# Raw-weight loads issued by ScalarE behind the upper-half copy, and a later place for the second block's first conversion step

## Chip, cores and metric

One core of one Trainium2 chip runs the whole kernel in one launch. The metric is the device time of one execution in microseconds (us).

## What is computed

```python
attn_out = _attn_ref(q, k, v)              # [2, 8, 576, 64]: pooled attention (factor 4) repeated, plus attention in a band |i-j| < 4
x = attn_out as [1152, 512]
h = x @ w_in; r = max(h, 0); g = s*r*r + b # d_ff = 2048
x = g @ w_out                              # [1152, 512]
p = probs / (sum(probs) + 1e-9)
for e in range(4):                         # d_ff = 1024 for each expert
    out += p[:, e:e+1] * (max(x @ w1[e], 0) @ w2[e])
```

The weights w_in and w_out of the first feed-forward network reach the kernel as pairs of 32-bit words, the bits of 64-bit floating-point numbers; the kernel makes 32-bit numbers of them.

## The kernel before

The work falls into three stages. The **attention** runs in 16 units, 4 groups of tokens by 4 pairs of heads, and each unit passes through a chain of short steps on several engines. The **first network** runs in four blocks (n = 0 to 3) of 512 columns of d_ff, the second in eight. TensorE does every large product as three products of fp32r parts: an upper part (a rounded copy) and a lower part (what the copy lost).

A unit's steps, with the lines: TensorE transposes q (L512), ScalarE copies it (L519 `qz`), VectorE pools it (L526 `qd`). TensorE computes the scores (L576 to L614), VectorE the row maxima (L615, L617), ScalarE the exponentials with their sums (L571, `exps`). VectorE normalises (L630 to L635), TensorE transposes the result (L657), ScalarE copies it (L660 `pT`), and TensorE multiplies by the values (L678 with the pooled values `vd`, L685). ScalarE and VectorE add the two results (L694 `ud`, L701 `xg`), ScalarE makes the upper part of x (L713) and GpSimd the lower one (L715; VectorE for the last unit of a group). `xg` has one buffer, so a unit's L701 waits for the previous unit's L713 and L715. GpSimd also pools the values (L474, L475). The steps of the units overlap: while one unit's exponentials run, the previous one is normalised and transposed.

From the fourth unit on, TensorE takes pieces of block 0 of the first network between these steps (`take_slot`); their results go through `L767` on ScalarE, `L769` on VectorE, `L772` on ScalarE and `L773` on VectorE. In the first ten units TensorE also multiplies a tile of zeros (L361, L584, `keep_warm`). The number of these multiplications is fixed in the program.

**Conversions.** Each block of the first network takes four quarters of weights, two of w_in and two of w_out, 1 MB each as raw words. `load_next` (L100) takes the next quarter from a list and issues its load into one of two `raw` buffers. A conversion (`prep`, L143) of a quarter has seven instructions over tiles of 128x1024: `magnitude` (L157, ScalarE), `clamp` (L161, VectorE), `join` (L167 and L175, VectorE), `sign` (L186, VectorE, the last reader of the raw words), `high` (L196, ScalarE) and `low` (L199, VectorE). The last two of a quarter are interleaved with the steps of the next one (`tail`, L203). There are 16 conversions, counted here from 1; conversions 1 to 4 serve block 0, 5 to 8 block 1. The first two loads are issued at the start; in the kernel before, `low` then calls `load_next`, which issues on SyncE's queue. A third load therefore waits until conversion 1's `sign` has read its raw buffer.

On every engine but GpSimd a scheduler sets the order of the instructions from the order in which the program issues them and from their priorities, so an edit at one place can move instructions at others. Each engine then runs its own list in order.

Of the kernel before, what the change touches and what calls it, by code (L numbers as in the profile page):

```python
# [8 lines left out]
F32 = mybir.dt.float32  # L9
# [3 lines left out]
ACTF = mybir.ActivationFunctionType  # L13
# [9 lines left out]
def attn_moe_moe_kernel(  # L23
# [14 lines left out]
    nc = tc.nc  # L38
# [40 lines left out]
    def f32(ap):  # L79
        return ap.bitcast(F32)  # L80
# [16 lines left out]
    tail = []  # L97
    pools = {}

    def load_next():  # L100
        if not stream:
            return
        n, which, half = stream.pop(0)
        wi, wo, f0 = blocks[n]
        m = 2 if n < n_moe1 else 1
        dt = I32 if n < n_moe1 else F32
        if n < n_moe1:
            wi, wo = wi.bitcast(I32), wo.bitcast(I32)
        f0 += half * 256
        if which == 0:  # L110
            src = wi[:, f0 * m : (f0 + 256) * m].rearrange("(k p) f -> p k f", p=P)
        else:
            src = wo[f0 : f0 + 256, :].rearrange("(c p) d -> p c d", p=P)
        if n < n_moe1:
            t = rawp.tile([P, 2048], dt, tag="raw", name="raw")
        else:
            if "raw2" not in pools:
                t = rawp.tile([P, 2048], dt, tag="raw", name="raw2")
                pools["raw2"] = [t[:, :1024], t[:, 1024:]]
            t = pools["raw2"].pop(0)  # L120
            pools["raw2"].append(t)
        nc.sync.dma_start(out=t.rearrange("p (a b) -> p a b", a=src.shape[1]), in_=src)
        raw[n, which, half] = t


# [2 lines left out]
    def w_slot(which):  # L128
        i = places[which].pop(0)
        places[which].append(i)  # L130
        if i < 3 - which:
            pool = wp1 if which else wp0
        else:
            pool = pools["wy" if which else "wx"]
        return [
            pool.tile([P, 1024], F32R, tag=f"w{which}{c}{i}", name=f"w{which}{c}", bufs=1)
            for c in range(2)
        ]

    def prep(n, which, half):  # L140

        if n >= n_moe1:
            return prep2(n, which, half)  # L143
        parts = w_slot(which)
        wt[n, which, half] = parts
        st = {}

        def words():
            w = raw[n, which, half].rearrange("p (n two) -> p n two", two=2)
            return w[:, :, 0], w[:, :, 1]  # L150

        def magnitude():
            f = rawp.tile([P, 1024], F32, tag="cv", name="cv")
            st["f"] = f
            nc.scalar.activation(out=f, in_=words()[1].bitcast(F32), func=ACTF.Abs)  # L157

        def clamp():
            f = st["f"]  # L160
            nc.vector.tensor_scalar(  # L161
                out=f, in0=f, scalar1=2.0**-15, scalar2=122879.9921875, op0=ALU.max, op1=ALU.min
            )

        def join():
            c = st["f"].bitcast(I32)
            nc.vector.tensor_scalar(  # L167
                out=c,
                in0=c,
                scalar1=5,  # L170
                scalar2=2,
                op0=ALU.logical_shift_left,
                op1=ALU.logical_shift_right,
            )
            nc.vector.scalar_tensor_tensor(  # L175
                out=c,
                in0=words()[0],
                scalar=29,
                in1=c,
                op0=ALU.logical_shift_right,  # L180
                op1=ALU.bitwise_or,
            )

        def sign():
            c = st["f"].bitcast(I32)
            nc.vector.scalar_tensor_tensor(  # L186
                out=c,
                in0=words()[1],
                scalar=-(2**30),
                in1=c,  # L190
                op0=ALU.bitwise_and,
                op1=ALU.bitwise_or,
            )

        def high():
            nc.scalar.copy(parts[0], st["f"])  # L196

        def low():
            nc.vector.tensor_tensor(  # L199
                out=parts[1], in0=st["f"], in1=f32(parts[0]), op=ALU.subtract  # L200
            )
            load_next()
            ready.add((n, which, half))  # L203


        nonlocal tail
        steps = [magnitude] + tail[:1] + [clamp] + tail[1:] + [join, sign]
        tail = [high, low]
        return steps

# [5 lines left out]
    def prep2(n, which, half):  # L216
# [10 lines left out]
        def done():  # L227
            load_next()
            ready.add((n, which, half))
# [118 lines left out]
    nc.vector.memset(idle, 0.0)  # L348

    last_pe = {}  # L350
    firsts = []

    def take_slot():
# [44 lines left out]
    def unit(u):  # L398
        g, j = divmod(u, NP)
        b, hf = divmod(g, HALVES)  # L400
        return g, j, b, hf
# [149 lines left out]
    def b_step(u):  # L551

        g, j, b, hf = unit(u)
# [14 lines left out]
        sm = sums[u % 2]  # L568

        def exps(out, ps, m, total):  # L570
            nc.scalar.activation(  # L571
                out=out, in_=ps, func=ACTF.Exp, bias=m, scale=1.0, accum_out=total
            )

# [41 lines left out]
        for a in range(len(pooled)):  # L616
            nc.vector.tensor_reduce(  # L617
                out=md[:, a], in_=pooled[a], axis=AX.X, op=ALU.max, negate=True
# [372 lines left out]
    for i in range(last + 1):  # L991
# [36 lines left out]
        if i < 2:  # L1028
            load_next()
# [104 lines left out]
```

## Time and profile before

| | |
|---|---|
| median of 3 runs | 686.23 us (685.72 to 687.32) |
| the profiled execution | 685.9 us |
| its span, first to last instruction | 684.1 us |
| TensorE busy | 673.0 us (98%) |
| VectorE busy | 404.7 us (59%) |
| ScalarE busy | 345.2 us (50%) |
| GpSimd busy | 103.0 us (15%) |

The time outside the span, 1.8 us, lies before the first and after the last instruction. Busy shares are means over the whole span; a stretch at the start may look quite different.

### The profile page before, as it was taken

The page shows a single profiled execution, that of the slowest core. Times are in us where ns is not written, and L with a number is a line of the kernel's source. Part 1 is how long each engine was busy: PE and PEld are TensorE (multiplying, and loading weights), DVE is VectorE, ACT ScalarE, POOL GpSimd, SP SyncE. Part 2 cuts the span into 40 slices and gives each one's busy share as a digit, 9 for nine tenths or more (in the row PEclk, how much of TensorE's full clock was granted, in tenths as well). Part 3 has the DMA queues.
Part 4 walks back from the last instruction along what each step waited for, and adds up shares of the span by engine and source line. Part 5 has one row for each costly group of instructions (what it writes and reads, how often), then busy time and mean ns, then how long its engine had stood idle before and what let it go on. Part 6 is the DMA issues. An engine that isn't in the chain of part 4 may idle for free.

```text
span 684.1 us, 11957 instructions
## 1 busy us (share of the span) xinstructions
PE 673.0 (98%) x4788; PEld 614.5 (90%) x4788; DVE 404.7 (59%) x720; ACT 345.2 (50%) x846; POOL 103.0 (15%) x123
## 2 busy tenths in 40 slices
PE   9879999999999999999999999999999999999997
PEld 6668888999999999999899998898998999988996
DVE  1899878598834425695525645646456365455442
ACT  3777788787956656754443433334234234343220
POOL 4431540100002001021201201210112012010000
PEclk9999999999999999999999999999999999999999
DMA  9975845133500101000301201101102012011012
GB/s 189 229 173 112 145 130 157 63 120 127 184 1 1 32 1 62 1 32 0 86 9 61 63 31 32 62 32 61 32 32 65 29 32 92 27 36 32 1 62 77
DMA packets 54167, 46.43 MB, mean 68 GB/s; under 512 B 32224, under 2 KB 42720, under 8 KB 54112
## 3 DMA queue, kind: packets, MB, share of 16 engines
q1 hardware_dynamic: 54112, 45.67, 24.5%
q8 instruction: 37, 0.61, 0.4%
q14 instruction: 18, 0.15, 0.1%
HBM read 43.31 MB, written 2.36 MB: 67 GB/s over the span
## 4 chain that ended last, share of the span: by engine, by line
PE 89%; DVE 7%; ACT 2%; issue 1%; POOL 1%; POOLq 0%; ACTq 0%
PE psm L316 43%; PE psx L863 26%; PE psx L316 13%; PE psa L361 2%; PE psa L591 1%; PE psa L657 1%; DVE cv L175 1%; PE psa L685 1%; PE psa L512 1%; DVE cv L167 1%; PE psa L494 1%; PE psa L678 1%; DVE cv L186 1%; DVE cv L161 0%; DVE pl L632 0%
## 5 line engine op out<-in xcount | busy, mean ns | idle before, releaser
L316 PE MATMUL psm<-w,h 128*128 128x512 f32 x864 | 208.7, 391 | 0.0
L316 PEld LDWEIGHTS psm<-w,h 128*128 128x128 f32 x864 | 158.5, 188 | 30.0
L863 PE MATMUL psx<-x,w 128*128 128x320 f32 (+1 forms) x768 | 117.7, 296 | 0.0
L863 PEld LDWEIGHTS psx<-x,w 128*128 128x128 f32 x768 | 109.2, 189 | 1.7
L259 POOL TENSOR_TENSOR sw<-raw 128x256 f32<-128x256 f32 x32 | 30.1, 960 | 412.1 <-DMA raw<-in_moe_w_dram 270.3
L878 ACT COPY r<-psx 128x320 f32<-128x320 f32 (+1 forms) x96 | 38.1, 396 | 92.9 <-PE psx L863 92.5
L881 ACT ACTIVATE h<-r 128x320 fp32r<-128x320 f32 (+1 forms) x96 | 42.1, 444 | 82.8 <-DVE r L892 82.8
L934 DVE SCALAR_TENSOR_TENSOR acc<-psm,pr,acc 128x512 f32<-128x512 f32 x63 | 47.2, 749 | 57.1 <-PE psm L316 57.1
L863 PE MATMUL psx<-t,w 128*128 128x320 f32 (+1 forms) x448 | 80.2, 302 | 0.3 <-DVE r L892 0.3
L892 DVE TENSOR_TENSOR r<-psx,r 128x320 f32<-128x320 f32 (+1 forms) x96 | 43.2, 456 | 57.9 <-PE psx L863 56.3
L863 PEld LDWEIGHTS psx<-t,w 128*128 128x128 f32 x448 | 67.0, 188 | 4.6 <-DVE r L892 0.6
L316 PE MATMUL psm<-x,w 128*128 128x320 f32 (+2 forms) x420 | 66.6, 310 | 0.0
L316 PEld LDWEIGHTS psm<-x,w 128*128 128x128 f32 x420 | 62.3, 189 | 0.3 <-issue 0.2
L882 DVE SCALAR_TENSOR_TENSOR h<-r,h 128x320 fp32r<-128x320 f32 (+1 forms) x96 | 48.2, 508 | 18.5 <-ACT h L881 16.4
L316 PE MATMUL psm<-h,w 128*128 128x256 f32 (+2 forms) x360 | 56.1, 305 | 0.3 <-DVE h L773 0.3
L316 PE MATMUL psx<-h,w 128*128 128x384 f32 (+1 forms) x312 | 55.8, 327 | 0.0
L316 PEld LDWEIGHTS psx<-h,w 128*128 128x128 f32 x312 | 52.0, 188 | 0.0
L316 PEld LDWEIGHTS psm<-h,w 128*128 128x128 f32 x360 | 50.9, 190 | 1.0 <-DVE h L773 0.5
L316 PE MATMUL psx<-x,w 128*128 128x384 f32 (+2 forms) x252 | 43.1, 320 | 0.0
L316 PEld LDWEIGHTS psx<-x,w 128*128 128x128 f32 x252 | 40.6, 188 | 0.0
L237 DVE TENSOR_TENSOR w<-raw,w 128x1024 fp32r<-128x1024 f32 x16 | 19.5, 1224 | 26.7 <-ACT w L234 26.7
L780 DVE TENSOR_TENSOR h<-r,h 128x384 fp32r<-128x384 f32 (+2 forms) x40 | 21.6, 541 | 20.9 <-ACT h L779 19.6
(105 smaller groups left out, 865.8 us busy)
## 6 DMA issues: line engine op xcount, KB each, us to landing
raw<-in_moe_w_dram SPq DMA_DIRECT2D x32, 512.0 KB
raw<-in_moe_w_in_dram SPq DMA_DIRECT2D x8, 1024.0 KB
raw<-in_moe_w_out_dram SPq DMA_DIRECT2D x8, 1024.0 KB
kn<-in_k_dram SPq DMA_DIRECT2D x8, 288.0 KB
v<-in_v_dram SPq DMA_DIRECT2D x8, 288.0 KB
out_dram<-acc SPq DMA_DIRECT2D x9, 256.0 KB
qn<-in_q_dram SPq DMA_DIRECT2D x8, 160.0 KB
vn<-in_v_dram SPq DMA_DIRECT2D x16, 72.0 KB
```

Of the source, the lines that this page charges most:

```text
L167: nc.vector.tensor_scalar(out=c, in0=c, scalar1=5, scalar2=2, op0=ALU.logical_shift_left, op1=ALU.logical_shift_right,)
L237: nc.vector.tensor_tensor(out=k0[1], in0=source(), in1=f32(k0[0]), op=ALU.subtract)
L259: nc.gpsimd.tensor_tensor(out=operand(out), in0=operand(x), in1=operand(y), op=op)
L316: nc.tensor.matmul(o, stat(ps, kk), mov(pm, kk, i), start=c == 0, stop=c == len(terms) - 1)
L361: nc.tensor.matmul(ps[:, c0:], idle[:, :P], idle[:, :n], start=True, stop=True)
L780: nc.vector.tensor_tensor(out=h[1], in0=r, in1=f32(h[0]), op=ALU.subtract)
L863: nc.tensor.matmul(ps, s_ap(n, half, a, w, kk), xt[x, pi][b][:, kk], start=first and c == 0, stop=c == len(terms) - 1, skip_group_check=True,)
L878: nc.scalar.copy(t, st[name])
L881: nc.scalar.activation(out=h[0][:, halves[hf]], in_=t, func=ACTF.Relu)
L882: nc.vector.scalar_tensor_tensor(out=h[1][:, halves[hf]], in0=t, scalar=0.0, in1=f32(h[0][:, halves[hf]]), op0=ALU.max, op1=ALU.subtract,)
L892: nc.vector.tensor_tensor(out=st[t], in0=st[name], in1=st[t], op=ALU.add)
L934: nc.vector.scalar_tensor_tensor(out=a, in0=ps, scalar=p_e, in1=a, op0=ALU.mult, op1=ALU.add)
```

## The change

`load_next` takes the engine that issues as an argument. `high` calls it with ScalarE, right behind its copy, and `low` no longer calls it. The first two loads, and those that `prep2` asks for (weights of the second network), stay on SyncE. `exps` keeps its instruction in `last_act["att"]`, and the `magnitude` of the second block (n == 1) is issued behind the latest of them.

```diff
--- before.py
+++ after.py
@@ -97,7 +97,7 @@
     tail = []
     pools = {}
 
-    def load_next():
+    def load_next(engine=nc.sync):
         if not stream:
             return
         n, which, half = stream.pop(0)
@@ -119,7 +119,7 @@
                 pools["raw2"] = [t[:, :1024], t[:, 1024:]]
             t = pools["raw2"].pop(0)
             pools["raw2"].append(t)
-        nc.sync.dma_start(out=t.rearrange("p (a b) -> p a b", a=src.shape[1]), in_=src)
+        engine.dma_start(out=t.rearrange("p (a b) -> p a b", a=src.shape[1]), in_=src)
         raw[n, which, half] = t
 
 
@@ -154,7 +154,8 @@
         def magnitude():
             f = rawp.tile([P, 1024], F32, tag="cv", name="cv")
             st["f"] = f
-            nc.scalar.activation(out=f, in_=words()[1].bitcast(F32), func=ACTF.Abs)
+            with tc.issue_after(last_act["att"].ins) if n == 1 else nullcontext():
+                nc.scalar.activation(out=f, in_=words()[1].bitcast(F32), func=ACTF.Abs)
 
         def clamp():
             f = st["f"]
@@ -194,12 +195,12 @@
 
         def high():
             nc.scalar.copy(parts[0], st["f"])
+            load_next(nc.scalar)
 
         def low():
             nc.vector.tensor_tensor(
                 out=parts[1], in0=st["f"], in1=f32(parts[0]), op=ALU.subtract
             )
-            load_next()
             ready.add((n, which, half))
 
 
@@ -348,6 +349,7 @@
     nc.vector.memset(idle, 0.0)
 
     last_pe = {}
+    last_act = {}
     firsts = []
 
     def take_slot():
@@ -568,7 +570,7 @@
         sm = sums[u % 2]
 
         def exps(out, ps, m, total):
-            nc.scalar.activation(
+            last_act["att"] = nc.scalar.activation(
                 out=out, in_=ps, func=ACTF.Exp, bias=m, scale=1.0, accum_out=total
             )
```

Line numbers grow by one from L157 on and by two from the end of `low` on, so L571 becomes L573 and L769 becomes L771. TensorE's list stays as it was up to the first products of block 0, and GpSimd's stays whole. ScalarE's list gets 16 loads, SyncE's loses them.

ScalarE's list around the fourth unit's exponentials (L571, `sum_107`); the rows L713 are the upper part of x, first of the first unit and then of the second, and L157 is conversion 2's first step. Before:

```order
L660 COPY pT<-psa 72x512
L713 CAST x_76<-xg 128x256
L157 ACTIVATE cv<-raw 128x1024
L571 ACTIVATE pl,sum_107<-psa,ml 128x72 x4
L571 ACTIVATE pd,sum_107<-psa,md 128x144
L660 COPY pT<-psa 72x256
L519 ACTIVATE qz<-psa 128x320
L694 ACTIVATE ud<-psa 128x64
L660 COPY pT<-psa 72x512
L196 CAST w_301<-cv 128x1024
L660 COPY pT<-psa 72x256
L713 CAST x_76<-xg 128x256
```

With the change, the same stretch, from the third load on; the first L158 is conversion 2's, the second conversion 3's:

```order
L122 DMA raw<-in_moe_w_out_dram 128x2x1024
L158 ACTIVATE cv<-raw 128x1024
L573 ACTIVATE pl,sum_107<-psa,ml 128x72 x4
L573 ACTIVATE pd,sum_107<-psa,md 128x144
L696 ACTIVATE ud<-psa 128x64
L662 COPY pT<-psa 72x512
L662 COPY pT<-psa 72x256
L521 ACTIVATE qz<-psa 128x320
L158 ACTIVATE cv<-raw 128x1024
L715 CAST x_76<-xg 128x256
L696 ACTIVATE ud<-psa 128x64
L662 COPY pT<-psa 72x512
```

Conversion 2's first step and the load that the program placed before it now stand ahead of the exponentials, the copies `pT` behind them, and x of the first unit (L715) behind conversion 3's first step.

VectorE's list where block 0 begins (`r` and `h` are block 0's; `sum_107` belongs to the normalisation of the sixth unit, `x_77` is the lower part of x of the fourth). Before, conversion 4 starts behind the first L769:

```order
L376 RECIPROCAL prs<-prs 128x9
L377 TENSOR_TENSOR pr<-pr,prs 128x36
L769 SCALAR_TENSOR_TENSOR r<-r,s_sb 128x256 x2
L161 TENSOR_SCALAR cv<-cv 128x1024
L773 SCALAR_TENSOR_TENSOR h<-r,b_sb,h 128x256 x2
L615 TENSOR_REDUCE ml<-psa 128x5
L769 SCALAR_TENSOR_TENSOR r<-r,s_sb 128x256
L617 TENSOR_REDUCE md<-psa 80x1 x2
L167 TENSOR_SCALAR cv<-cv 128x1024
L773 SCALAR_TENSOR_TENSOR h<-r,b_sb,h 128x256
L175 SCALAR_TENSOR_TENSOR cv<-raw,cv 128x1024
```

With the change, the same stretch ends a conversion's fourth step (L187, conversion 4) ahead of the normalisation, and its last (L201) ahead of the first L771:

```order
L187 SCALAR_TENSOR_TENSOR cv<-raw,cv 128x1024
L633 RECIPROCAL sum_107<-sum_107 128x7
L378 RECIPROCAL prs<-prs 128x9
L634 TENSOR_TENSOR pl<-pl,sum_107 128x360
L637 TENSOR_TENSOR pd<-pd,sum_107 80x288
L703 TENSOR_TENSOR xg<-psa,ud 128x256
L379 TENSOR_TENSOR pr<-pr,prs 128x36
L617 TENSOR_REDUCE ml<-psa 128x5
L717 TENSOR_TENSOR x_77<-xg,x_76 128x256
L619 TENSOR_REDUCE md<-psa 80x1 x2
L201 TENSOR_TENSOR w_306<-cv,w_305 128x1024
L771 SCALAR_TENSOR_TENSOR r<-r,s_sb 128x256 x2
```

All five VectorE steps of conversion 4 thus stand ahead of block 0's first elementwise work, and the conversions of the second block, which stood right behind, have gone further down the list, between exponentials of later groups.

## Rows read from the trace of the kernel before

**Rows 1.** Windows, core 0: us, busy (count) of each engine, granted clock, DMA share, GB/s
```profile
20.00:40.00 20.00, 18.20 (x250) 14.38 (x248) 18.75 (x34) 14.01 (x48) 8.99 (x9) 1.00 0.81 181
40.00:60.00 20.00, 16.48 (x206) 13.86 (x204) 17.98 (x38) 14.70 (x62) 3.88 (x3) 1.00 0.59 151
60.00:80.00 20.00, 20.00 (x255) 17.15 (x252) 19.60 (x38) 16.81 (x53) 7.30 (x7) 1.00 0.90 175
80.00:132.00 52.00, 51.62 (x652) 45.52 (x650) 37.61 (x85) 39.90 (x154) 16.70 (x19) 1.00 0.44 125
132.00:680.00 548.00, 547.70 (x3288) 510.51 (x3287) 304.56 (x510) 251.59 (x511) 57.64 (x64) 1.00 0.15 47
```

**Rows 2.** Timeline of TensorE, 23 to 175: start, us, instruction, idle before and releaser
```profile
33.02 0.46 PE L678 MATMUL psa<-pT,vd 72*64 72x64 f32 x8 [1.40 <-ACT pT L660]
...
41.76 0.41 PE L657 MATMUL psa<-ident,pd 128*72 128x128 f32 x2 [1.31 <-ACT pd L571]
...
49.59 0.30 PE L657 MATMUL psa<-ident,pl 128*72 128x128 f32 x1 [2.03 <-DVE qd L526]
...
49.96 4.55 PE L316 MATMUL psm<-x,w 128*128 128x256 f32 x36
...
126.88 0.50 PE L316 MATMUL psm<-h,w 128*128 128x256 f32 x2 [0.27 <-DVE h L773]
...
134.79 11.37 PE L316 MATMUL psm<-x,w 128*128 128x320 f32 x72
```

**Rows 3.** Groups by line, a conversion's seven: busy, mean ns, idle before and releaser
```profile
L175 DVE SCALAR_TENSOR_TENSOR cv<-raw,cv 128x1024 int32<-128x1024 int32 x16 | 20.9, 1306 | 0.3
...
L186 DVE SCALAR_TENSOR_TENSOR cv<-raw,cv 128x1024 int32<-128x1024 int32 x16 | 19.4, 1214 | 0.0
L199 DVE TENSOR_TENSOR w<-cv,w 128x1024 fp32r<-128x1024 f32 x16 | 19.4, 1220 | 1.5 <-ACT w L196 1.5
...
L157 ACT ACTIVATE cv<-raw 128x1024 f32<-128x1024 f32 x16 | 18.3, 1146 | 0.1
...
L196 ACT CAST w<-cv 128x1024 fp32r<-128x1024 f32 x16 | 16.7, 1052 | 1.8 <-DVE cv L186 1.8
...
L167 DVE TENSOR_SCALAR cv<-cv 128x1024 int32<-128x1024 int32 x16 | 12.4, 772 | 0.3
...
L161 DVE TENSOR_SCALAR cv<-cv 128x1024 f32<-128x1024 f32 x16 | 11.8, 739 | 4.4 <-ACT cv L157 4.1
```

**Rows 4.** Timeline of ScalarE, 26 to 56
```profile
29.57 0.40 ACT L713 CAST x<-xg 128x256 fp32r<-128x256 f32 x1 [0.45 <-DVE xg L701]
29.88 1.14 ACT L157 ACTIVATE cv<-raw 128x1024 f32<-128x1024 f32 x1
...
39.74 0.32 ACT L571 ACTIVATE pl<-psa,ml 128x72 f32<-128x72 f32 x1 [0.53 <-DVE md L617]
...
47.82 0.32 ACT L571 ACTIVATE pl<-psa,ml 128x72 f32<-128x72 f32 x1 [0.62 <-DVE md L617]
```

**Rows 5.** Timeline of VectorE, 28 to 80, first steps of conversions 2, 3 and 5
```profile
31.05 1.50 DVE L161 TENSOR_SCALAR cv<-cv 128x1024 f32<-128x1024 f32 x1
...
39.76 0.68 DVE L161 TENSOR_SCALAR cv<-cv 128x1024 f32<-128x1024 f32 x1
40.47 1.63 DVE L167 TENSOR_SCALAR cv<-cv 128x1024 int32<-128x1024 int32 x1
...
62.34 0.69 DVE L161 TENSOR_SCALAR cv<-cv 128x1024 f32<-128x1024 f32 x1 [0.21 <-ACT cv L157]
```

**Rows 6.** Timeline of GpSimd, one pooling step of the values
```profile
30.74 1.26 POOL L474 TENSOR_TENSOR v<-v 72x512 f32<-72x512 f32 x1
```

**Rows 7.** Timeline of SyncE's queue, issues of two loads of raw weights
```profile
24.59 0.39 SPq L122 DMA_DIRECT2D raw<-in_moe_w_out_dram  x1
...
36.68 0.89 SPq L122 DMA_DIRECT2D raw<-in_moe_w_out_dram  x1
```

**Rows 8.** Window in which one load of raw weights runs, issued at 103.61
```profile
103.60:108.10 4.50, 4.50 (x49) 3.88 (x48) 2.45 (x7) 3.31 (x12) 0.73 (x1) 1.00 0.79 266
```

## The prediction

> **What bounds the kernel now.** I read the table of engine shares first: TensorE is busy for 673.0 of the 684.1 us span, so it is idle for only 11.1 us in all. The edit adds and removes no TensorE instruction, and the multiplications by zeros are fixed in number too. Unless TensorE's own instructions change speed, a gain can come only from those 11.1 us. Then the windows show where they lie [rows 1]. From 20 to 40 TensorE is busy for 18.20 of 20 us and from 40 to 60 for 16.48, so 1.80 + 3.52 = 5.3 us are idle there; from 60 to 80 none, and from 132 to 680 only 548.00 - 547.70 = 0.3 us. The granted clock is 1.00 in every row, the higher level of 2.4 GHz, so nothing is to be had from the clock.
>
> Next the timeline names the waits [rows 2]: 1.40 us at 33.02 for a copy `pT`, 1.31 at 41.76 and 2.03 at 49.59 around the fifth and sixth units' exponentials, and much later 0.27 for an `h` at 126.88. The first three are 4.7 of the 5.3 us. They all end on one circle of short steps: maxima on VectorE, exponentials on ScalarE, normalisation on VectorE, transposes on TensorE, `pT` on ScalarE. Between 20 and 60 VectorE is busy for 18.75 and 17.98 of 20 us [rows 1]: VectorE is what is scarce there, and the conversions share it. ScalarE's exponentials at 39.74 and 47.82 were ended by VectorE's maxima L617 after idle times of 0.53 and 0.62 us [rows 4], so these two wait for VectorE.
>
> So the question is what the edit does to ScalarE's and VectorE's lists before 60 us. After that the stretch has to become worse before it matters.
>
> **The loads, moved from SyncE to ScalarE.** One issue takes 0.39 us on SyncE's queue, once 0.89 [rows 7]. No row of before has ScalarE issue such a load, so I bound the price there by 0 (the issue overlaps other work) and 0.89, and take 0.39, the commoner: 16 x 0.39 = 6.2 us more on ScalarE. ScalarE has room: it is busy for 14.01, 14.70 and 16.81 of 20 us in the three early windows [rows 1] and for 345.2 us of the whole. Only one load stands directly ahead of work that TensorE waits for, the third load, ahead of conversion 2's first step and the fourth unit's exponentials; I carry it below.
>
> What the loads gain is nothing that was waited for. Conversions begin when L157 has a turn on ScalarE; its group has 0.1 us of idle time in 16 instructions, none of it put down to a load [rows 3]. SyncE issued the third load at 24.59; by the new order it stands behind other work on ScalarE and is issued near 28.0. A load of this size, issued at 103.61, was over by 108.1, at 266 GB/s [rows 8], so it takes some 4.5 us alone. Issued at 28.0 to 28.4 it should be in by 33.5, conversion 3's first step comes up at 33.7 by the chain below, and there is no margin for a second delay. If it is late by a whole extra load time because other transfers run beside it, that is up to 4.5 us on ScalarE, ahead of the fifth unit's exponentials: a rival below. The issue itself costs the path 0 to 0.89 us, inside the next term.
>
> By the rows the issuing engine's time is all that the loads change. By the Trainium skill, page "DMA: Bandwidth & Descriptors", section "Issuing engines are not separate DMA queues", loads from several engines run on the same 16 DMA engines and interleave, so another issuer saves issue time alone. No run here shows it yet; it speaks against a gain from more parallel transfers, and the sum would stay as it is.
>
> **Conversion 2 ahead of the fourth unit's exponentials.** Before, ScalarE ran L713 at 29.57 and L157 at 29.88 for 1.14 us, and the exponentials followed at 31.04. Now it runs the load (28.0 to 28.4), L158 (to 29.55) and then these exponentials, which wait for the fourth unit's maxima on VectorE, unmoved. They begin near 30.9, no later than before. But `ud` and both copies `pT` now stand behind them, of which the 512-wide one ran ahead of L157 before. TensorE's L678 of the third unit then starts at about 33.5 instead of 33.02: **+0.5 us** (0 if the copies fall into the time in which TensorE waits for them already, 1.14 if they are late by a whole L157).
>
> **x of the first unit later.** L713 moves from 29.57 to about 35.0, behind conversion 3's first step. GpSimd's subtraction and its pooling L474 and L475 follow it, in GpSimd's unchanged order, so they slide by 5 us. That moves a collision. While L474 ran at 30.74 [rows 6], VectorE's L161 at 31.05 took 1.50 us, and the next conversion's, at 39.76 with GpSimd between two instructions, took 0.68; L167 at 40.47, beside the next L474, took 1.63 [rows 5], against a mean of 0.77 [rows 3]. So a VectorE step beside GpSimd's pooling loses about 0.8 us, and with the slide it is conversion 3's first steps that lose it, directly ahead of the fifth unit's maxima. `xg` has one buffer, so the next L701 also waits for GpSimd's subtraction; by the chain VectorE stands idle there for about 0.65 us. Counting both, the exponentials of 39.74 start at 41.2 to 42.9, and TensorE's wait at 41.76 ends 1.3 to 3.0 us later. I take 2, between the ends, since the collision may fall on one step or on two.
>
> By the Trainium skill, page "SBUF — State Buffer", section "🔬 SBUF: two separate sides", VectorE and GpSimd share a pair of ports that one of them holds alone. Hence two clashes would cost what they cost wherever they fall, and the slide alone would cost nothing; the trace's 1.50 beside 0.68 agrees with the lock.
>
> **What is given back.** Between the fifth unit's and the sixth unit's exponentials (39.74 and 47.82) VectorE has the same work to do before and after, about 7.7 us of it, and two items cost less now: GpSimd's next L474 has moved away from it, which saves L167 its slow form (1.63 against a mean of 0.77, so 0.9, and perhaps as much again on the step behind it), and ScalarE's idle time of 0.62 ahead of the sixth unit's exponentials can close. So the sixth unit's exponentials start at 47.3 to 48.6, against 47.82. TensorE's wait at 49.59, 2.03 us long, was put down to a VectorE step `qd`; the new order frees the bank with an exponential instead, so that it ends between 49.15 and 50.5. The shift of TensorE at 50 us is then -0.45 to +1.0, and I take **+0.4**. The two earlier shifts, of 0.5 and of 2, are in it, not added to it: the later wait takes them up.
>
> **Conversion 4 ahead of block 0's first work.** Before, its L161 stood behind the first L769. Now five steps, 0.74 + 0.77 + 1.31 + 1.21 + 1.22 = 5.25 us of VectorE work [rows 3], stand ahead of it, some of it ahead of the sixth unit's normalisation. TensorE covers this with the 36 products at 49.96, 4.55 us long, of which nine come later in the new order. By my chain of mean durations x of the fourth unit is then ready near 56.2, and TensorE wants it near 56.2. With no cover left, the whole 5.25 us would be exposed; with cover for all of it, nothing. The row it is nearest to is the 4.55 us of covered products, so I take **+0.2**.
>
> **Blocks 0 and 1 behind 60 us.** Two conversions of the second block, 2 x 5.25 = 10.5 us of VectorE work, leave the stretch that begins at 62.34 [rows 5]. VectorE was busy there for 19.60 of 20 us, but TensorE for 20.00 [rows 1]: nothing waited, so the relief is worth nothing. By the new order the work comes back near 98 to 115, and conversions 7 and 8 near 125 to 140. VectorE is busy there for 37.61 of 52 us and later for 304.56 of 548 [rows 1], which leaves it room; block 1's first products begin at 134.79 and fill 11.37 us [rows 2] before its second layer wants the quarters 7 and 8. I cost this at 0; without that slack it would be a conversion's length, 5.25. The wait of 0.27 at 126.88 may go: **0**, bounds -0.27 and +1.
>
> **The sum.** 685.9 + 0.4 + 0.2 + 0 = 686.5 for an execution like the profiled one. Its median of runs is 686.23, 0.3 higher, so I forecast **686.8**. The measurement can tell a difference of about 0.2%, 1.37 us, so this is no change. The terms' ends, -0.45 - 0.3 and 1.0 + 1.0, place this case between 685.5 and 688.2, by the median.
>
> **The rivals.** *Faster.* The list that is new from 28 to 50 may remove the waits themselves: if conversion 2 done 1.3 us earlier pulls both later pairs of maxima forward, the waits 1.31 and 2.03 shrink. Both gone would be 686.2 - 3.3 = 682.9; half of them, 684.6. For it speaks that these waits end on VectorE; against it, that VectorE's own work before 50 us is not reduced: the second block's conversions that leave stood behind 62 us. 0.24.
>
> *Slower.* Conversion 3's first step blocks ScalarE until its load is in. That decides when the third load lands over 1 us after 33.7; ScalarE then holds `ud`, `pT` and the fifth unit's exponentials alike, these are late by 3 us or more, and the 2.03 us wait at 49.59 can't take it all up. The price is 1.4 to 3 us, so 687.6 to 689.5; the landing without margin speaks for it, the 2.03 us at 49.59 that can shrink against. 0.28.
>
> *The change does nothing.* If the scheduler gave the same lists, the time would be 686.2. The lists differ at the places shown, so this is part of the middle case, 0.48 in all.
>
> **How the numbers follow.** Faster by over 0.2% 0.24, within 0.2% 0.48, slower 0.28. The range of 684.0 to 689.6 leaves out the deep ends of both rivals, about 0.1 each.
>
> **What would show it.** In the new profile: `pT` behind the exponentials and L678 at about 33.5; L717 on GpSimd near 35.3 and L162 beside it slow; the wait near 42 to 44 longer than 1.31; the one near 49.5 shorter than 2.03; TensorE dense from 60. The forecast is wrong if TensorE's idle time from 20 to 60 falls below 4 us or passes 6.7, if a first step of a conversion waits for its load, or if block 1's first products wait.

## The result and the profile after

| | before | changed |
|---|---|---|
| median | 686.22 us (685.72 to 687.32, 4 runs) | 694.18 us (691.77 to 698.67, 4 runs) |
| ratio to before, 95% interval | | 1.0123 (1.0094 to 1.0153) |
| profiled execution, its span | 685.9, 684.1 us | 698.67, 696.7 us |
| TensorE busy, idle in the span | 673.0, 11.1 us | 681.2, 15.5 us |

The changed kernel is slower by about 8 us; 686.8 was forecast, within 684.0 to 689.6. The profiled execution is the slowest of the four: it shows the places well and the size too large.

The row of busy times of the changed kernel:

```profile
PE 681.2 (98%) x4788; PEld 619.9 (89%) x4788; DVE 406.8 (58%) x720; ACT 340.4 (49%) x846; POOL 102.7 (15%) x123
```

The 12.6 us between the two spans are 4.4 us of idle time and 8.2 us in which TensorE was busy longer with the same 4788 instructions. The windows of the changed kernel (us, busy and count of PE, PEld, DVE, ACT, POOL, granted clock, DMA share, GB/s) say why:

```profile
20.00:40.00 20.00, 17.84 (x214) 13.37 (x213) 15.85 (x29) 13.18 (x45) 6.34 (x7) 0.91 0.85 197
40.00:60.00 20.00, 15.34 (x137) 12.46 (x138) 16.79 (x33) 10.57 (x41) 5.27 (x5) 0.66 0.70 172
60.00:80.00 20.00, 20.00 (x250) 17.16 (x249) 10.85 (x28) 13.27 (x52) 3.14 (x4) 1.00 0.66 149
...
100.00:120.00 20.00, 18.29 (x180) 15.84 (x180) 15.44 (x30) 13.15 (x44) 8.03 (x6) 0.91 0.27 80
```

The granted clock fell to 0.91, 0.66 and 0.91, where it had been 1.00 in every window [rows 1]. In windows of 1 us it stands at 0.50, the 1.2 GHz level, from 35 to 38, from 45 to 58 and from 114 to 116. TensorE, dense in 60 to 80, has a second gap after 100. Its timeline names the waits:

```profile
32.93 0.46 PE L680 MATMUL psa<-pT,vd 72*64 72x64 f32 x8 [1.98 <-ACT pT L662]
...
46.81 0.64 PE L659 MATMUL psa<-ident,pd 128*72 128x128 f32 x2 [4.44 <-ACT pd L573]
...
57.07 4.11 PE L317 MATMUL psm<-x,w 128*128 128x256 f32 x27
...
111.45 0.56 PE L317 MATMUL psm<-h,w 128*128 128x320 f32 x2 [1.53 <-DVE h L775]
```

The first wait was 1.40 us [rows 2] and is 1.98; the second, 1.31 at 41.76, is 4.44 and ends at 46.81; the third, 2.03, is gone, and block 0 starts at 57.07 instead of 49.96; an `h` of block 0 is late by 1.53 us at 111.45. What ScalarE, VectorE and GpSimd did ahead of the 4.44 us, one fence each (L158 is conversion 3's first step, L162 and L168 its next two, L715 and L717 the parts of the first unit's x, L703 the next `xg`, L632 and L637 steps of the fourth unit's normalisation, L476 GpSimd's pooling of the values, L617 and L619 the fifth unit's maxima, L573 its exponentials):

```profile
25.89 0.42 ACTq L122 DMA_DIRECT2D raw<-in_moe_w_out_dram  x1
...
35.51 1.13 ACT L158 ACTIVATE cv<-raw 128x1024 f32<-128x1024 f32 x1 [2.30 <-DMA raw<-in_moe_w_out_dram]
36.54 0.40 ACT L715 CAST x<-xg 128x256 fp32r<-128x256 f32 x1
...
44.79 0.32 ACT L573 ACTIVATE pl<-psa,ml 128x72 f32<-128x72 f32 x1 [4.95 <-DVE md L619]
```

```profile
37.77 0.42 DVE L703 TENSOR_TENSOR xg<-psa,ud 128x256 f32<-128x256 f32 x1 [2.90 <-POOL x L717]
38.11 0.88 DVE L632 TENSOR_SCALAR sum<-sum 128x7 f32<-128x7 f32 x1
38.91 0.68 DVE L162 TENSOR_SCALAR cv<-cv 128x1024 f32<-128x1024 f32 x1
...
39.62 1.10 DVE L168 TENSOR_SCALAR cv<-cv 128x1024 int32<-128x1024 int32 x1
...
41.54 1.36 DVE L637 TENSOR_TENSOR pd<-pd,sum 128x144 f32<-128x144 f32 x1
...
43.97 0.52 DVE L617 TENSOR_REDUCE ml<-psa 128x5 f32<-128x360 f32 x1
44.41 0.50 DVE L619 TENSOR_REDUCE md<-psa 80x1 f32<-80x144 f32 x2
```

```profile
37.01 0.72 POOL L717 TENSOR_TENSOR x<-xg,x 128x256 fp32r<-128x256 f32 x1 [8.54 <-ACT x L715]
37.69 1.27 POOL L476 TENSOR_TENSOR v<-v 72x512 f32<-72x512 f32 x1
...
41.27 1.47 POOL L476 TENSOR_TENSOR v<-v 72x512 f32<-72x512 f32 x1
```

VectorE before, at the same steps:

```profile
36.39 0.41 DVE L701 TENSOR_TENSOR xg<-psa,ud 128x256 f32<-128x256 f32 x1
36.73 0.16 DVE L630 TENSOR_SCALAR sum<-sum 128x7 f32<-128x7 f32 x1
...
37.53 0.30 DVE L635 TENSOR_TENSOR pd<-pd,sum 128x144 f32<-128x144 f32 x1
```

ScalarE issued the third load at 25.89 and L158 started at 35.51: it had waited 2.30 us for that load, 9.6 us behind the issue. L715, behind it in ScalarE's list, ran at 36.54, GpSimd's L717 at 37.01, and VectorE stood still for 2.90 us until `xg` was free again. `xg` itself is only 1.38 us later than before (37.77 against 36.39). The rest is VectorE's work ahead of the maxima: conversion 3's L162 and L168, 0.68 + 1.10 = 1.78 us, stood behind them before [rows 5], and steps beside GpSimd's pooling are longer, L632 0.88 us against 0.16 and L637 1.36 against 0.30. The maxima came at 43.97 and the exponentials at 44.79, 5.05 us later than before [rows 4]. TensorE's 4.44 us are the end of that chain.

How much of it is the wait for the load? The six profiled executions in which ScalarE issues it (the kernels are described below) have waits of different length there (us):

| | before | after_again | after_filled_wait | after_filled_again | changed | act_loads_no_hold | third_load_on_act |
|---|---|---|---|---|---|---|---|
| conversion 3's first step waits for its load | 0 | 1.05 | 1.32 | 1.60 | 2.30 | 2.32 | 2.44 |
| from the fourth to the fifth unit's exponentials | 8.70 | 13.20 | 13.50 | 13.74 | 14.43 | 14.46 | 14.55 |

Each us of waiting adds about 1 us. Carried on to no waiting at all, the second row would stand near 12.1, an estimate from these six. So of the 5.7 us that the changed kernel loses between the two exponentials (5.05 above, since its fourth unit's came 0.7 us earlier), about 2.3 are the wait for the load and about 3.4 the new order of the steps.

### The profile page after: what moved, and what is told of

It is laid out like the page before. It is cut to its first block, busy times and chain, and to the rows that moved or that the text cites. A ratio compares the mean times of both kernels' runs of the same rounds, so it can differ in the third digit from the quotient of the medians.

```text
span 696.7 us, 11934 instructions
## 1 busy us (share of the span) xinstructions
PE 681.2 (98%) x4788; PEld 619.9 (89%) x4788; DVE 406.8 (58%) x720; ACT 340.4 (49%) x846; POOL 102.7 (15%) x123
## 4 chain that ended last, share of the span: by engine, by line
PE 88%; DVE 5%; ACT 3%; DMA 2%; issue 1%; POOL 0%; ACTq 0%
PE psm L317 41%; PE psx L865 25%; PE psx L317 13%; PE psa L363 2%; DMA raw<-in_moe_w_out_dram 1%; PE psa L659 1%; PE psa L593 1%; ACT pl L573 1%; PE psa L687 1%; DMA kn<-in_k_dram 1%; PE psa L514 1%; DVE r L771 1%; PE psa L496 1%; PE psa L680 1%; DVE pl L634 0%
## 5 line engine op out<-in xcount | busy, mean ns | idle before, releaser
L317 PE MATMUL psm<-h,w 128*128 128x256 f32 (+2 forms) x360 | 58.1, 310 | 1.7 <-DVE h L775 1.5
```

The lines of the kernel that those rows point to most:

```text
L317: nc.tensor.matmul(o, stat(ps, kk), mov(pm, kk, i), start=c == 0, stop=c == len(terms) - 1)
```

## Experiments

Ratios are to the kernel before on the same chip, with 95% intervals. Line numbers differ by a few from kernel to kernel. The second table says where in the attention the time goes: for some of the 16 units, the start of TensorE's product with `vd` (L678 before) in the kernel's timeline less that in the kernel before, in us. A kernel's start alone shifts such a number by 1 to 2 us, so the steps within a row are what counts.

| kernel | median us (runs) | ratio |
|---|---|---|
| hold_only | 692.82 (4) | 1.0094 (1.0074 to 1.0114) |
| act_loads_no_hold | 694.63 (4) | 1.0133 (1.0107 to 1.0159) |
| sync_loads_no_hold | 690.83 (4) | 1.0079 (1.0054 to 1.0105) |
| sync_loads_hold | 696.03 (4) | 1.0150 (1.0135 to 1.0165) |
| third_load_on_act | 689.20 (10) | 1.0050 (1.0031 to 1.0069) |
| third_load_on_sync | 689.06 (7) | 1.0032 (1.0012 to 1.0053) |
| hold_second_only | 689.02 (6) | 1.0039 (1.0026 to 1.0053) |
| after_filled_wait | 695.74 (4) | 1.0125 (1.0103 to 1.0148) |
| sync_high_from_block_1 | 686.28 (10) | 1.0000 (0.9991 to 1.0009) |
| fourth_load_early | 684.35 (12) | 0.9975 (0.9962 to 0.9987) |
| loads_4_to_6_early | 685.13 (12) | 0.9985 (0.9976 to 0.9995) |
| loads_4_and_5_early | 684.56 (9) | 0.9981 (0.9970 to 0.9992) |
| after_again | 696.55 (5) | 1.0126 (1.0105 to 1.0147) |
| after_filled_again | 695.49 (4) | 1.0129 (1.0112 to 1.0146) |

| unit (start before) | 2 (33.02) | 4 (45.43) | 5 (58.27) | 10 (94.00) | 12 (108.39) | 16 (130.80) |
|---|---|---|---|---|---|---|
| changed | -0.09 | 7.36 | 6.56 | 7.78 | 12.54 | 12.20 |
| hold_only | -1.02 | -0.83 | -1.04 | -0.72 | 4.31 | 3.89 |
| act_loads_no_hold | -0.28 | 6.10 | 3.05 | 7.70 | 8.88 | 8.93 |
| sync_loads_no_hold | -1.31 | -1.31 | 2.92 | 3.23 | 3.66 | 3.65 |
| sync_loads_hold | -1.06 | -0.80 | 4.81 | 4.99 | 10.29 | 9.88 |
| third_load_on_act | -0.41 | 4.66 | 2.51 | 2.88 | 3.33 | 3.33 |
| third_load_on_sync | -0.89 | -0.73 | -3.15 | 1.46 | 2.65 | 2.70 |
| hold_second_only | -1.55 | -1.53 | -0.05 | -0.26 | -0.11 | 2.30 |
| fourth_load_early | -1.29 | -1.03 | -1.88 | -1.75 | -1.79 | -1.79 |
| after_filled_again | -0.59 | 4.06 | 5.46 | 5.67 | 8.95 | 8.61 |

### The parts of the change, one by one

The hold alone, in the kernel before (with `last_act` as in the change):

```diff
-            nc.scalar.activation(out=f, in_=words()[1].bitcast(F32), func=ACTF.Abs)
+            with tc.issue_after(last_act["att"].ins) if n == 1 else nullcontext():
+                nc.scalar.activation(out=f, in_=words()[1].bitcast(F32), func=ACTF.Abs)
```

> The kernel before with the held first step of the second block alone; loads stay on SyncE. Theory (two costs: the third load, issued by ScalarE, lands late and stops ScalarE at conversion 3's first step; the hold puts two conversions in front of block 0's h): only the second cost is here, a wait of about 1.5 us near 110 and some lower clock behind it, none at 40 to 47, so 687 to 690 us. Rival (the hold is the whole cost, the loads nothing): 692 to 695 us. Rival (the loads are the whole cost): 685.5 to 687 us.

The changed kernel without the hold:

```diff
-            with tc.issue_after(last_act["att"].ins) if n == 1 else nullcontext():
-                nc.scalar.activation(out=f, in_=words()[1].bitcast(F32), func=ACTF.Abs)
+            nc.scalar.activation(out=f, in_=words()[1].bitcast(F32), func=ACTF.Abs)
```

> The changed kernel without the hold: ScalarE issues the loads behind its upper-half copy. Theory of two costs: the DMA wait of ScalarE at conversion 3's first step stays (2 to 3 us), TensorE waits 4 to 5 us near 45 and the granted clock falls behind it; no wait near 110, so 689 to 693 us. Rival (the hold is the whole cost): 685 to 688 us. Rival (the loads are the whole cost): 692 to 696 us.

The same with the load in `high` on SyncE, without and with the hold:

```diff
         def high():
             nc.scalar.copy(parts[0], st["f"])
-            load_next(nc.scalar)
+            load_next()
```

> The call of the load moved from the lower-half step to the upper-half step, but still issued by SyncE, no hold. ScalarE's list up to 47 us is that of before. Theory: nothing waits for these loads, so 685.5 to 687.5 us, clock 0.998 or more. Rival (an earlier place of the loads is what hurts, whoever issues): above 689 us, with a first step of a conversion waiting for its load.

> The changed kernel with one word undone: SyncE issues the loads instead of ScalarE; the place in the upper-half step and the hold stay. Theory of two costs: as the hold alone, 687 to 690 us, with the wait for an h near 110. Rival (the hold is the whole cost): 692 to 695 us. Rival (the loads on ScalarE are the whole cost): 685.5 to 687 us.

Every part alone is slower than the kernel before, by 4.9 to 8.7 us, and the parts don't add up. My theory of two costs placed both but undersized both, and the hold alone (692.82) lies where the rival put it; that rival falls by the two kernels without the hold. The other rival, that the loads are the whole cost, has its time in the kernel without the hold (694.63) and falls by the hold alone. Loads on SyncE (690.83) were expected to cost nothing; they came out where the rival had them, but no first step of a conversion waited for its load, so its reason falls too. With both (696.03) the time is above every expectation. There are three costs, at three places.

**The hold costs at the 12th unit**: -0.72 to 4.31 in its row, 4.99 to 10.29 with the loads on SyncE. The profiled execution of the hold alone is the fastest of its four (690.34), so its row shows less than the median. VectorE in the hold alone (L176 and L187 are conversion 5's, L771 and L775 make block 0's `r` and `h`), and the same two rows before (L769, L773):

```profile
98.53 1.22 DVE L176 SCALAR_TENSOR_TENSOR cv<-raw,cv 128x1024 int32<-128x1024 int32 x1
99.66 1.03 DVE L771 SCALAR_TENSOR_TENSOR r<-r,s_sb 128x320 f32<-128x320 f32 x1
100.62 2.29 DVE L187 SCALAR_TENSOR_TENSOR cv<-raw,cv 128x1024 int32<-128x1024 int32 x1
102.83 1.01 DVE L775 SCALAR_TENSOR_TENSOR h<-r,b_sb,h 128x320 fp32r<-128x320 f32 x1
```

```profile
98.50 0.79 DVE L769 SCALAR_TENSOR_TENSOR r<-r,s_sb 128x320 f32<-128x320 f32 x1 [0.61 <-ACT r L767]
...
99.92 0.88 DVE L773 SCALAR_TENSOR_TENSOR h<-r,b_sb,h 128x320 fp32r<-128x320 f32 x1
```

Conversion 5 used to run near 62 us. Held, it stands among block 0's elementwise steps: L176 goes first and `r` starts at 99.66 instead of 98.50, L187 takes 2.29 us ahead of `h`, against a mean of 1.21 [rows 3] and with a pooling step of GpSimd from 100.31 beside it, and `h` starts at 102.83 instead of 99.92. The changed kernel has the same four steps with the same durations from 106.07 on. TensorE had no wait there before:

```profile
101.34 0.42 PE L317 MATMUL psm<-h,w 128*128 128x320 f32 x1 [1.13 <-ACT h L774]
...
103.89 0.56 PE L317 MATMUL psm<-h,w 128*128 128x320 f32 x2 [1.52 <-DVE h L775]
...
104.88 1.07 PE L659 MATMUL psa<-ident,pl 128*72 128x128 f32 x4
```

1.13 + 1.52 = 2.65 us of waiting, and then a lower clock: a transposition L659 of four at 104.88 takes 1.07 us, against 0.60 at full clock.

**The call in `high` costs at the 5th unit** on SyncE: -1.31 to 2.92. TensorE and ScalarE there in the kernel with all loads on SyncE:

```profile
48.58 0.32 PE L658 MATMUL psa<-ident,pl 128*72 128x128 f32 x1 [2.33 <-ACT pd L572]
...
52.68 4.75 PE L316 MATMUL psm<-x,w 128*128 128x256 f32 x27 [1.26 <-ACT x L714]
```

```profile
48.77 1.14 ACT L157 ACTIVATE cv<-raw 128x1024 f32<-128x1024 f32 x1
...
52.23 0.41 ACT L714 CAST x<-xg 128x256 fp32r<-128x256 f32 x1 [0.98 <-DVE xg L702]
```

Conversion 4's first step, at 53.40 in the kernel before, stands at 48.77, ahead of ScalarE's copies for the sixth unit; VectorE's L161 and L167 run at 50.18 and 51.18, ahead of `xg`, so x is late and TensorE waits 1.26 us for it, with a half clock around it.

**The third load on ScalarE costs at the 4th unit**: -0.28 to 6.10, the chain shown above; its wait for `pd` is 4.45 us without the hold too. With only this load back on SyncE (689.06, 1.0032, below) instead of all on ScalarE (694.63, 1.0133), most of the loss is gone. Later the kernel with all loads on ScalarE and no hold loses again, between the units 5 and 10, with conversions 5 and 6 near 68 and 74:

```profile
46.65 0.41 PE L658 MATMUL psa<-ident,pd 128*72 128x128 f32 x2 [4.45 <-ACT pd L572]
...
84.71 0.46 PE L513 MATMUL psa<-ident,qn 64*128 64x64 f32 x4 [0.53 <-DVE xg L702]
...
89.60 0.46 PE L605 MATMUL psa<-kd,qd 64*64 64x144 f32 x4 [1.18 <-POOL kd L542]
...
110.45 0.63 PE L658 MATMUL psa<-ident,pl 128*72 128x128 f32 x4 [0.98 <-DVE pl L633]
```

These waits, for `xg`, `kd` and `pl`, are not in the changed kernel, which with the hold is no slower than without. That conversions 5 and 6 stand there isn't enough to cause them: in loads_4_to_6_early they start at 61.8 and 67.8, as in third_load_on_sync (62.2 and 68.3), which has waits of 0.53 for `xg` and 1.19 for `kd`, and there is neither. The loads from the seventh on, which SyncE issues in loads_4_to_6_early and ScalarE in the others, are a cause left; that isn't shown.

### The third load

ScalarE issues this load alone, or all but this one (of the kernel with loads in `high`, no hold):

```diff
-            load_next(nc.scalar)
+            load_next(nc.scalar if (n, which, half) == (0, 0, 0) else nc.sync)   # third_load_on_act
+            load_next(nc.sync if (n, which, half) == (0, 0, 0) else nc.scalar)   # third_load_on_sync
```

> Loads called from the upper-half step and issued by SyncE, except the third load (the one behind conversion 1), which ScalarE issues; no hold. Theory (this one load, landing some 9 us after its issue, stops ScalarE at conversion 3's first step): ScalarE waits about 2.3 us for it near 33 to 35, TensorE waits 4 to 5 us near 46 and the clock falls to 0.5 there; 692 to 696 us, like all loads on ScalarE. Rival (the 13 other loads on ScalarE carry the cost): no such wait, 689 to 691.5 us, like all loads on SyncE.

> The mirror image: ScalarE issues all loads behind its upper-half copy except the third, which SyncE issues; no hold. Theory: ScalarE's list up to conversion 3 is that of before, no wait for a load near 34, TensorE's wait near 41 stays 1.3 us or less; 687 to 691.5 us. Rival (the other loads on ScalarE carry the cost): 692 to 696 us.

ScalarE's conversion 3 and TensorE's next wait, with this one load on ScalarE:

```profile
35.34 1.15 ACT L157 ACTIVATE cv<-raw 128x1024 f32<-128x1024 f32 x1 [2.44 <-DMA raw<-in_moe_w_out_dram]
```

```profile
45.22 0.41 PE L658 MATMUL psa<-ident,pd 128*72 128x128 f32 x2 [3.00 <-DVE qd L527]
```

The place is shown: one load moved makes ScalarE wait 2.44 us and shifts the 4th unit by 5.1 us (-0.41 to 4.66). The expected 692 to 696 us are missed: 689.20 is where the rival had it, though the wait that the rival excluded is there. 2.15 us come back at the 5th unit, and no later load stands in ScalarE's way. All loads on SyncE took no less (1.0079 against 1.0050), so in this pair the load's cost doesn't show in the median. With only this load on SyncE there is no wait for it, and block 0 starts early:

```profile
47.54 0.30 PE L658 MATMUL psa<-ident,pl 128*72 128x128 f32 x1 [0.71 <-DVE qd L527]
...
47.91 3.48 PE L316 MATMUL psm<-x,w 128*128 128x256 f32 x27
```

The wait of 2.03 us [rows 2] is 0.71 there, and block 0 starts at 47.91; the loss comes after that unit. 689.06 is as expected, and the rival (692 to 696) falls.

Did ScalarE's issue make the load slow? The traces' DMA packets of this load, 256 of 4096 bytes, say no. They end 9.0 us behind the issue in the changed kernel and 7.8 to 9.0 in all six traces with ScalarE's issue; with SyncE's they end 5.4 us behind it in the kernel before, and 8.7 (third_load_on_sync), 9.0 (sync_loads_no_hold) and 9.6 (hold_only) in others, within 5.4 to 10.8 in all ten. What differs is when ScalarE comes to conversion 3's first step: at 36.5 to 38.0 where SyncE issues, over 2 us after the last of these packets, and at 33.2 in the changed kernel, 1.7 us ahead of it. The changed order with SyncE's issue wasn't run.

### The hold on conversion 6 alone

From the kernel with the hold alone:

```diff
-            with tc.issue_after(last_act["att"].ins) if n == 1 else nullcontext():
+            with tc.issue_after(last_act["att"].ins) if (n, which, half) == (1, 0, 1) else nullcontext():
```

> The kernel before with the hold on the second of the second block's two conversions (conversion 6) alone; conversion 5 stays near 62 us. Theory (conversion 5's steps on VectorE ahead of block 0's r and h near 100 make TensorE wait 2.6 us, and the clock falls behind that): no wait for h, or one below 0.6 us, 685.2 to 688 us. Rival (any conversion held into the third group costs the same): waits of 1 us or more near 100 to 110, 689 to 693 us.

The 4 us at the 12th unit are gone (-0.26 to -0.11), so conversion 5 caused them. The time, 689.02, is still above what I expected and at the edge of the rival's range, without the rival's waits near 100 to 110: the row rises by 1.5 us at the 5th unit, of which more below, and from -0.11 to 2.30 at the last units, with a wait for another `h`:

```profile
128.68 0.50 PE L317 MATMUL psm<-h,w 128*128 128x256 f32 x2 [0.83 <-ACT h L774]
```

### The lower clock

36 multiplications of zeros where TensorE waits 4.4 us, put into a free bank ahead of the transposes of `pd`:

```diff
         while cols:
+            if u == 3 and c0:
+                spare = mm_bank()
+                for _ in range(36):
+                    with tc.issue_after(last_pe["att"].ins):
+                        nc.tensor.matmul(spare[:, :256], idle[:, :P], idle[:, :256], start=True, stop=True)
             ps = bank()
```

> The changed kernel with 36 multiplications of zeros of 256 columns added on TensorE where it waits 4.4 us for the fifth unit's exponentials; they take about 0.11 us each, 3.9 us in all, so they fill the wait and add little to it. Theory (a good part of the loss is the lower clock that follows the wait): the granted clock from 44 to 59 stays 1.00, some 6 us of TensorE time come back: 686 to 690.5 us. Rival (the loss is the waiting itself, the clock is a by-product of the profile): 692 to 696 us.

The theory missed, and the time is where the rival put it. The clock was 1.00 in all of this profile, and the time was 695.74, with 693.49 and 695.91 at a mean clock of 0.999. Since the changed kernel's own runs spread over 7 us, both ran again on one chip.

> The changed kernel again, beside the next one on one chip. Its four runs so far spread from 691.8 to 698.7 us at mean clocks from 0.985 to 0.994. Expected: 691 to 698 us, median 693 to 696.

> The changed kernel with the filled wait again, same multiplications. Theory now (the clock costs part of the loss, the rest is the late exponentials, which the fill can't mend): clock 0.995 or more, median 1 to 4 us below the changed kernel of this call. Rival (TensorE at half speed is covered by ScalarE's and VectorE's chain, so the clock costs nothing): within 1 us of the changed kernel, or above it.

695.49 (694.92 to 696.96) against 696.55 (693.62 to 699.62): 1.1 us, within the spread, where the two expectations meet; the clock, 0.992 to 0.994, stayed below the expected 0.995. The profile of the filled kernel shows where TensorE waits (L664 is L657 of before):

```profile
45.62 0.41 PE L664 MATMUL psa<-ident,pd 128*72 128x128 f32 x2 [0.23 <-ACT pd L573]
...
53.65 0.43 PE L664 MATMUL psa<-ident,pl 128*72 128x128 f32 x1 [2.03 <-ACT pd L573]
...
107.88 0.42 PE L317 MATMUL psm<-h,w 128*128 128x320 f32 x1 [1.27 <-ACT h L779]
```

The fill takes the wait at 45.62 down to 0.23, and then the wait for the sixth unit's `pd`, which the slow TensorE of the changed kernel had covered, is back with 2.03 us. So most of the time at half clock from 45 to 58 lay beside ScalarE's and VectorE's late chain. What the clock costs by itself in the changed kernel stays open. In the ten runs of third_load_on_act, the five at a mean clock of 0.997 or more took 687.73 to 689.25 us and the five at 0.993 or less 689.15 to 692.86, but a longer wait may be behind both.

Two other traces show it alone. Up to 70 us, hold_second_only runs the lists of the kernel before with the same waits of TensorE (1.40, 1.31 and 2.02 us), but its clock stands at 0.50 from 49.3 to 52.7. Block 0's 36 products, 4.55 us before [rows 2], take 1.5 us longer, and its row goes from -1.53 to -0.05:

```profile
48.42 6.03 PE L317 MATMUL psm<-x,w 128*128 128x256 f32 x36
```

In sync_high_from_block_1, described below, the instructions of all four engines stand in the order of the kernel before, and the clock is at 0.50 from 33.8 to 37.2. The third unit is 1.6 us later by that (-0.53 to 1.09), and the next waits, 0.17 and 1.80 us for 1.31 and 2.03 before, take it up (-0.58 at the 5th unit). So 3.4 us at half clock cost 1.5 us where TensorE had no wait to come, and nothing ahead of one.

### A version that beats both

The early start of block 0 in third_load_on_sync suggests moving only loads that no step of ScalarE waits for. From the kernel before:

```diff
         def high():
             nc.scalar.copy(parts[0], st["f"])
+            if (n, which, half) in [(0, 0, 1)]:
+                load_next(nc.scalar)
...
-            load_next()
+            if (n, which, half) not in [(0, 0, 1)]:
+                load_next()
```

> The kernel before with one load changed: the fourth, issued by ScalarE behind conversion 2's upper-half copy instead of by SyncE behind its lower half. The kernel with the third load on SyncE was 2 us ahead of the kernel before at the seventh unit and lost it later; this keeps the early part of it. Theory (ScalarE may issue a load where its list isn't stopped by one, and an earlier conversion 4 then uses VectorE time ahead of block 0's start): 684 to 686.5 us. Rival (any earlier conversion 4 pushes block 0 as with the loads on SyncE): 688 to 691 us.

The two others put (0, 1, 0), and (0, 1, 0) and (0, 1, 1), into the list as well.

> The fourth and fifth loads behind the upper-half copies on ScalarE, all others as before. Expected between the two others of this call: by theory 684 to 686.5 us, by the rival 687 to 690 us.

> As the fourth load early, and the fifth and sixth loads too, all behind the upper-half copies on ScalarE; from the seventh on as before. Theory: ScalarE's and VectorE's lists up to 60 us are those of the kernel with the third load on SyncE, 2 us ahead there, and the later losses (waits for xg, kd and pl between 75 and 105) do not come if the seventh load's issue caused them: 683.5 to 686 us. Rival (conversions 5 and 6, begun earlier, cause them): 687 to 690 us.

With all loads on SyncE and no hold, only those from block 1 on called from `high`:

```diff
-            load_next(nc.scalar)
+            if n:
+                load_next()
```

> All loads on SyncE; block 0's four conversions call the next load from the lower-half step as before, the twelve later ones from the upper-half step; no hold. Theory (the cost of the earlier call on SyncE is conversion 4 alone, ahead of the sixth unit's normalisation and block 0's first results near 50): 685.2 to 687.2 us, no wait above 2.1 us near 50 and none for an x. Rival (the later loads cost too): 688 us or more.

All three early versions beat the kernel before on the one chip where they ran, the fourth load alone by 0.25%, 684.35 us. ScalarE waits there too, but only 0.27 us, for conversion 4's load at 42.49. Waits and windows of fourth_load_early (L660 is L657 of before):

```profile
31.73 0.46 PE L681 MATMUL psa<-pT,vd 72*64 72x64 f32 x8 [1.39 <-ACT pT L663]
...
40.75 0.41 PE L660 MATMUL psa<-ident,pd 128*72 128x128 f32 x2 [1.06 <-ACT pd L574]
...
47.47 0.30 PE L660 MATMUL psa<-ident,pl 128*72 128x128 f32 x1 [0.94 <-DVE qd L529]
```

```profile
20.00:40.00 20.00, 17.81 (x247) 14.07 (x244) 19.07 (x35) 14.24 (x50) 9.31 (x9) 1.00 0.98 219
40.00:60.00 20.00, 18.10 (x216) 15.34 (x216) 19.92 (x39) 16.28 (x59) 2.90 (x3) 1.00 0.78 191
```

TensorE is busy for 18.10 of 20 us from 40 to 60, against 16.48 [rows 1], at a clock of 1.00; the wait of 2.03 is 0.94. Within its row, though, this kernel gains only 0.5 us (-1.29 to -1.79); the other 1.3 us lie ahead of the second unit, so where most of the 1.85 us of the medians comes from isn't shown. The later loads called from `high` on SyncE cost nothing (686.28), and the four engines' lists are those of the kernel before, so the earlier calls in block 0 carry that cost.

## Why the prediction was wrong, point by point

- **"It takes some 4.5 us alone ... it should be in by 33.5."** This step failed. The estimate came from a load that ran beside almost nothing [rows 8]. The third load was issued at 25.89, not at 28.0, among loads of q and v, and let ScalarE go on at 35.5: 9.6 us, of which 9.0 to its last packet. ScalarE came to conversion 3's first step at 33.2, close to the 33.7 of the forecast, and waited 2.30 us. In the DMA table of the changed kernel ScalarE's loads are a second queue (kind: packets, MB, share of 16 engines):

```profile
q1 hardware_dynamic: 47968, 29.94, 16.9%
q10 hardware_dynamic: 6144, 15.73, 6.8%
```

  By the Trainium skill, page "DMA: Bandwidth & Descriptors", section "Issuing engines are not separate DMA queues", loads from two engines interleave on the same 16 DMA engines; the traces agree that the second issuer bought no time, with 7.8 to 9.0 us to the last packet against 5.4 to 10.8 on SyncE. The kernel before had the 5.4, and came to conversion 3 at 38.03, so its trace gave no warning.
- **"x of the first unit later ... I take 2."** The mechanism was right and the term too small: by the estimate above the new order alone made the fifth unit's exponentials about 3.4 us later, beyond the 1.5 to 3.2 us that I allowed them (41.2 to 42.9 for 39.74), and with the wait for the load 5.7. The collision with GpSimd's pooling did not fall on L162, which took 0.68 us, as in the clear; it fell on L632, L168 and L637.
- **The slower rival** had this mechanism, its place and its condition, with a chance of 0.28 and 1.4 to 3 us. The load came 1.8 us behind the 33.7 I set. The price was wrong, since I let ScalarE's delay count once. It came on top of the new order, through L715, GpSimd's L717 and the one buffer of `xg`, where VectorE stood still for 2.90 us (forecast 0.65).
- **"What is given back" (+0.4)**: block 0 started 7.1 us late. The wait at 49.59 was taken up, as I said, but 2 us of slack can't hold 5 us.
- **Conversion 2 ahead of the exponentials (+0.5)**: right in size; the first wait grew from 1.40 to 1.98 (the product at 33.02 is the second unit's, not the third's).
- **Conversion 4 (+0.2)**: right in the changed kernel, where block 0 shows no wait for x behind it, but only because TensorE was late anyhow. With the loads on SyncE the same place costs 4.2 us.
- **"Blocks 0 and 1 behind 60 us": 0.** This step failed. I compared busy shares of VectorE and the due time of the converted weights, and didn't look at what the moved conversion would stand in front of. It stood in front of an `h`: 1.53 us of waiting in the changed kernel, 2.65 us and 6.9 us of the median with the hold alone. I had named 5.25 us as the price if the slack were missing, here and for conversion 4, but the ends of the sum counted +1 at most for the two.
- **"Nothing is to be had from the clock"** looked at a gain only. The kernel before sits at 1.00 with waits up to 2.03 us; the changed one fell to 0.50 at its waits of 1.98, 4.44 and 1.53 us, and TensorE was busy for 8.2 us longer in the profiled execution, much of it covered.
- **The signs of being wrong** came true: TensorE's idle time from 20 to 60 was 2.16 + 4.66 = 6.8 us, past the 6.7 named, and a first step of a conversion waited for its load.

## What to carry to other kernels

Ask of a step that is moved what will stand behind it on its engine, even where that engine is half idle: here two steps of a conversion, 3.5 us ahead of one `h`, made TensorE wait 2.65 us though VectorE had room for them elsewhere. Take a load's time from a stretch as crowded as the one it moves into, and from more than one execution: the same load took 5.4 us in one trace and up to 10.8 in others. And when a load moves to another engine, look where the step that needs it lands in the lists: here the step came some 4 us earlier and the load did not, and by the estimate above the order alone cost more than the wait. The one load moved with hardly any wait behind it (0.27 us) was worth 0.25%.

## What was not expected of the hardware

- The granted clock fell to 0.50 for 3 to 14 us at or behind waits of 1.2 to 4.4 us. But the kernel before kept 1.00 through waits of 1.40, 1.31 and 2.03 us, and in the hold alone and in sync_high_from_block_1, whose lists are the same up to there, it fell at 33 us behind the same wait of 1.40 us; so the length of the last wait doesn't decide it.
- ScalarE's issue of a load took 0.37 to 0.46 us, as most of SyncE's did [rows 7], and twice more: 1.08 (fourth_load_early) and 1.14 (loads_4_and_5_early). SyncE's took up to 1.81.
- One load of 1 MB, the third, took 5.4 to 10.8 us from issue to last packet in sixteen traces, whichever engine issued it.
